# A fused attention and mixture kernel: first expert product in two halves, first steps and last outputs in another order

## The chip, the cores and the metric

The kernel runs on one core of a Trainium2 chip. Its time is the device time of one execution in microseconds; the median of several runs counts. TensorE (PE) multiplies, VectorE (DVE), ScalarE (ACT) and GpSimd (POOL) work on tiles, and SyncE (SP) issues the transfers. PEld is TensorE's loading of weights.

## What is computed

The reference is an attention with a narrow window and block summaries, followed by a soft mixture of experts on its output. Cut to what matters:

```python
# attention: 4 batches, 8 heads, 768 positions, head size 64; blocks of 32, window 16
k_sum = k.reshape(B, H, nb, block, D).max(axis=3)
v_sum = v.reshape(B, H, nb, block, D).mean(axis=3)
scores_l = scale * (q @ k^T), only where |i - j| < 16
scores_s = scale * (q @ k_sum^T) + log(32)
a = softmax(concat(scores_l, scores_s))
x = a @ concat(v, v_sum)                      # 3072 rows of 512

# mixture: 8 experts with 4 slots each, hidden size 1024
logits = x @ phi                              # 3072 x 32
slot_input = softmax(logits, axis=0).T @ x    # 32 x 512
h = relu(slot_input[e] @ w1[e])               # per expert, 4 x 1024
slot_out[e] = h @ w2[e]                       # 4 x 512
out = softmax(logits, axis=1) @ slot_out      # 3072 x 512
```

## The kernel before

Each engine executes its instructions in the order in which the program's text issues them; nothing reorders them. Engines wait for each other by semaphores.

The attention runs in 24 steps. A step is one third of the positions (256) of one half of a batch's heads; three steps share a key tile `kk` (two tiles, used in turn). Step i does the scores of step i on PE (line 234), their masked maxima on DVE (`soft_max`, line 253: eight operations that write p and its row maximum m), the exponentials on ACT (line 263, and line 265 after a subtraction on POOL, line 269), transposes (line 275) and their copies (line 280) for step i-1, and the product with v (line 291) for step i-2.

A key tile holds, beside the keys, the maxima of each block of 32 keys and the 16 keys at each edge. `k_max` forms the block maxima (DVE, line 187), `k_put` copies them into the tile (line 210), and `k_edge` copies the edges (line 203). The scores need all three. For the first tile k_put ran on DVE, for all others on POOL. `v_sum` (the words V0 to V7 of the table PLAN) sums v in blocks: 48 small products on PE (line 327), a copy `vp` on ACT and an addition into `vsst` on DVE (line 340). `put_v` then copies vsst into a v tile on POOL (line 350), and the product with v waits for that. PLAN says for each step which of such pieces are begun, ahead of the mark | within the step or behind it at its end.

`load_piece` transfers the expert weights, 512 KB each, 32 pieces of w1 and 32 of w2, into buffers as they come free, on SP's queue. From the sixth step on they run beside the attention.

Behind the attention the softmax over positions is finished (`lanes`, `slots`), and then the softmax over slots runs on DVE in two parts (lines 646 to 660), while PE multiplies with w1: 32 pieces of four products each into one result `hps` (line 667). The result is clipped at zero on DVE (`hs`), transposed on PE (`ph`, line 681) and copied into the two tiles W1ST and W2ST on DVE (line 683). Then comes w2 in three groups of columns: a (256), b and c (128 each). `stage2` is a generator: 16 steps of a or 8 of b or c on PE (line 705), the scaling `sos` on DVE (line 715), a product that adds up four parts (line 718) and a copy into `sls` on DVE (line 720). `combine` makes the outputs of a block of 128 columns from sls: A stands for the first two blocks, B for the third and C for the fourth. For each block it makes four products of 256 columns, copied by ACT and DVE into one 512 KB piece, and four of 512, copied into two pieces (lines 731, 742, 747), each then issued on SP's queue. The text END is the order at the end: each of its words advances one of these generators by one step; a digit is for reading only.

## Time and profile before

| | |
|---|---|
| median of three runs | 193.09 us (191.21 to 193.2) |
| the profiled execution | 191.26 us |
| its span | 189.0 us |
| PE busy | 165.9 us, 88% |
| DVE busy | 121.1 us, 64% |
| ACT busy | 94.4 us, 50% |
| POOL busy | 71.9 us, 38% |
| moved by DMA | 66.35 MB, 351 GB/s over the span |

The span runs from the first to the last instruction of the profiled execution; the time of an execution is longer by what lies around it. A share of busy time is a mean over stages that have different limits.

### The profile page before, as it was taken

The numbers are of one execution on the slowest core, as the hardware profiler recorded it, in microseconds if no ns is written. First come the engines' busy times: TensorE is split into PE (matmuls) and PEld (weight loads), VectorE is DVE, ScalarE is ACT, GpSimd is POOL, SyncE is SP. The second block draws the span as 40 slices with busy tenths as digits, with TensorE's granted clock in tenths as the row PEclk, the third lists the DMA queues.
The fourth block names the chain that finished last, engine by engine and source line by source line (L and its number), as shares of the span: only waits on it lengthen the run. The fifth ranks groups of instructions, "written<-read, shape, count | busy, mean of one in ns | idle before, by whom it ended". The sixth has DMA issues, their size and how long they took to land.

```text
span 189.0 us, 7987 instructions
## 1 busy us (share of the span) xinstructions
PE 165.9 (88%) x3201; PEld 130.0 (69%) x3201; DVE 121.1 (64%) x626; ACT 94.4 (50%) x244; POOL 71.9 (38%) x147
## 2 busy tenths in 40 slices
PE   6596999998999979899999898989779989998940
PEld 5394877976968967697798696878357755664720
DVE  1758599686879688848978885864567610135450
ACT  2026667587676677756678577765301000033240
POOL 3425956748544943824854844420020000000000
PEclk9969999999999999999999999999999999999985
DMA  5999989998799998979899999979999999999697
GB/s 193 415 401 400 344 336 299 385 393 312 223 368 386 304 355 262 352 231 297 290 264 389 402 408 408 388 275 394 416 409 404 402 413 408 406 401 396 251 397 269
DMA packets 20628, 66.35 MB, mean 351 GB/s; under 512 B 2288, under 2 KB 2288, under 8 KB 20592
## 3 DMA queue, kind: packets, MB, share of 16 engines
q1 hardware_dynamic: 20448, 65.48, 93.0%
q8 instruction: 25, 0.41, 0.9%
q10 hardware_dynamic: 144, 0.37, 0.5%
q14 instruction: 11, 0.09, 0.1%
HBM read 59.55 MB, written 6.29 MB: 348 GB/s over the span
## 4 chain that ended last, share of the span: by engine, by line
PE 55%; DVE 12%; ACT 12%; issue 4%; POOL 3%; DMA 2%; DVEq 1%; POOLq 0%; ACTq 0%; SPq 0%
PE s L234 8%; PE o L291 8%; PE pt L275 8%; PE hps L667 7%; PE so L705 6%; PE pp L327 5%; DVE p L253 5%; ACT xt L364 4%; PE pp L361 3%; ACT ptr L280 3%; PE op L731 3%; DMA out<-wa 2%; ACT p L263 2%; PE pp L374 2%; PE pp L417 2%
## 5 line engine op out<-in xcount | busy, mean ns | idle before, releaser
L263 ACT ACTIVATE p<-p,m 128x128 f32<-128x128 f32 x100 | 32.0, 391 | 27.3 <-DVE m L253 27.3
L253 DVE CUSTOM_DVE_ANT_0 p<-s,cs 128x128 f32<-128x128 f32 x192 | 42.6, 286 | 4.4 <-PE s L234 4.1
L269 POOL TENSOR_TENSOR p<-m,p 128x512 f32<-128x512 f32 x23 | 23.9, 1038 | 44.0 <-DVE m L253 28.1
L234 PE MATMUL s<-kk,q 64*64 64x128 f32 x768 | 29.9, 280 | 4.2 <-DVE kk L210 2.2
L350 POOL COPY v<-vsst 24x520 f32<-24x520 f32 x48 | 29.4, 612 | 4.4 <-issue 1.6
L234 PEld LDWEIGHTS s<-kk,q 64*64 64x64 f32 x768 | 24.0, 136 | 10.2 <-issue 4.7
L291 PE MATMUL o<-v,ptr 120*64 120x65 f32 (+1 forms) x768 | 27.9, 225 | 1.5 <-DVE x L312 0.9
L291 PEld LDWEIGHTS o<-v,ptr 120*64 120x64 f32 (+1 forms) x768 | 24.6, 138 | 5.6 <-issue 4.6
L275 PE MATMUL pt<-ident,p 128*128 128x128 f32 x192 | 27.9, 282 | 0.6 <-ACT p L265 0.2
L280 ACT COPY ptr<-pt 128x512 f32<-128x512 f32 x47 | 24.7, 571 | 1.7 <-PE pt L275 1.7
L275 PEld LDWEIGHTS pt<-ident,p 128*128 128x128 f32 x192 | 20.4, 140 | 6.2 <-issue 3.3
L187 DVE TENSOR_REDUCE ks<-kk 128x8 f32<-128x256 f32 x48 | 17.0, 410 | 4.3 <-DMA kk<-kx 4.2
L265 ACT ACTIVATE p<-p 128x512 f32<-128x512 f32 x23 | 14.7, 639 | 8.8 <-POOL p L269 8.7
L312 DVE TENSOR_TENSOR x<-o,z 128x256 f32<-128x256 f32 x48 | 18.1, 419 | 0.8
L253 DVE DVE_READ_ACCUMULATOR2_ANT m<- 128x1 f32 x192 | 15.9, 83 | 0.0
L327 PE MATMUL pp<-v,cs 64*64 64x128 f32 x384 | 14.0, 284 | 0.8 <-ACT xt L364 0.7
L327 PEld LDWEIGHTS pp<-v,cs 64*64 64x64 f32 x384 | 12.0, 141 | 1.6 <-ACT xt L364 1.2
L361 PE MATMUL pp<-ident,x 128*128 128x128 f32 x88 | 11.6, 273 | 0.1
L309 DVE TENSOR_SCALAR z<-o 128x8 f32<-128x8 f32 x24 | 4.0, 165 | 11.8 <-PE o L291 11.2
L364 ACT COPY xt<-pp 128x512 f32<-128x512 f32 x21 | 11.4, 595 | 0.0
L203 POOL COPY kk<-kk 128x192 f32<-128x192 f32 x32 | 9.6, 342 | 4.3 <-DMA kk<-kx 4.3
L742 ACT COPY wa<-op 128x256 f32<-128x256 f32 (+1 forms) x3 | 1.2, 445 | 20.0 <-PE op L731 20.0
(134 smaller groups left out, 199.9 us busy)
## 6 DMA issues: line engine op xcount, KB each, us to landing
wa<-w SPq DMA_DIRECT2D x40, 512.0 KB, 7.7
v<-vx SPq DMA_DIRECT2D x24, 520.0 KB, 6.1
kk<-kx SPq DMA_DIRECT2D x16, 400.0 KB, 5.3
q<-qx SPq DMA_DIRECT2D x24, 256.0 KB, 4.8
v<-w SPq DMA_DIRECT2D x7, 512.0 KB, 6.2
kk<-w SPq DMA_DIRECT2D x6, 512.0 KB, 6.9
x<-w SPq DMA_DIRECT2D x5, 512.0 KB, 7.5
out<-v SPq DMA_DIRECT2D x3, 512.0 KB, 4.8
```

Source lines behind the costliest of these rows:

```text
L234: nc.tensor.matmul(s[r][64 * c : 64 * c + 64, u, :].rearrange("p (a k) -> p a k", a=2), lhsT=qb[64 * r : 64 * r + 64, i % NQR, pr, o : o + ...
L253: nc.vector.tensor_tensor_reduce(out=p[:, u, :], in0=s[:, u, :], in1=maskv[:, mk, :], scale=-0.125, scalar=-NEG, op0=ALU.add, op1=ALU.min, ...
L263: nc.scalar.activation(out=p[:, u, :], in_=p[:, u, :], func=AF.Exp, scale=-1.0, bias=m[:, u : u + 1])
L269: nc.gpsimd.tensor_tensor(out=p, in0=m.unsqueeze(2).broadcast_to([128, 4, 128]), in1=p, op=ALU.subtract)
L275: nc.tensor.transpose(pt[:, u, :], p[:, u, :], ident)
L280: (eng or nc.scalar.copy)(out=ptr, in_=ptr_[i, r])
L291: nc.tensor.matmul(o[64 * c : 64 * c + 64, r, u, :], lhsT=ptr[0:K, u, 64 * c : 64 * c + 64], rhs=v[0:K, c, tt, 2 * pr + r, :], start=True, ...
L312: nc.vector.tensor_tensor(out=x[:, r], in0=o[:, r, :, 0:64].rearrange("p (t q) d -> p t q d", t=2), in1=z[:, r].rearrange("p (t q) -> p t ...
L327: nc.tensor.matmul(pv[c][64 * g : 64 * g + 64, 0:128].rearrange("p (h d) -> p h d", h=2), lhsT=cs[64 * c : 64 * c + 64, o : o + 64], rhs=v ...
L350: eng.tensor_copy(out=vs[i % NV][n0 : n0 + NB, c].rearrange("n t h c -> n t (h c)"), in_=src.broadcast_to([NB, 2, 260]))
L361: nc.tensor.transpose(pv[:, 128 * c : 128 * c + 128], x, ident)
L364: (nc.vector.tensor_copy if on_dve else nc.scalar.copy)(out=xt.rearrange("p c t -> p (c t)"), in_=pv)
```

## The change

At the start, the first key tile's block maxima are copied for two of six tiles of positions by DVE and for four by POOL, ahead of POOL's memset of W1ST. The q tile of step 1 is loaded ahead of the first v tiles. V0 moves from the end of step 0 into step 1; the put_v of the first v tile follows it. The block maxima of the second key tile move to the end of step 1 and into step 2, and k_put and k_edge of that tile follow POOL's subtraction of step 2.

At the experts, the product with w1 is split into experts 0 to 3 and 4 to 7. Each half has its own result and is clipped, transposed and copied by a generator `hidden`. The first half's transposes stand behind the 20th piece, the second half's behind the fourth step of a (the new word h in END). The second part of the softmax over slots moves behind the 20th piece. In END, block B's outputs begin before the last three steps of c.

```diff
--- before.py
+++ after.py
@@ -39,7 +39,7 @@
 
 
 PLAN = {
-    0: "| V0",
+    1: "V0 |",
     2: "| V1",
     5: "| V2",
     6: "X0 X1 |",
@@ -66,8 +66,8 @@
 
 CHUNKS = {"a": (0, 256), "b": (256, 128), "c": (384, 128)}
 END = (
-    "a a a a a a a a a a a a a a a a a1 b b a2 b b a3 b b A A b A A b A A c A A c b1 c b2 c b3 c "
-    "c c c c1 B c2 c3 B B B C C C C"
+    "a a a a h a a a a a a a a a a a a a1 b b a2 b b a3 b b A A b A A b A A c A A c b1 c b2 c b3 c B c B c "
+    "B c c1 B c2 c3 C C C C"
 )
 
 
@@ -202,13 +202,14 @@
                 src = bass.AP(src.tensor, src.offset, [src.ap[0], src.ap[1], [128, NTT], [1, 16]])
                 eng.tensor_copy(out=e[:, :, :, 16 * half : 16 * half + 16], in_=src)
 
-    def k_put(hb, eng):
+    def k_put(hb, eng, t0=0, n=NTT):
         if hb >= HB:
             return
         for c in range(2):
             o = 0 if c else 32
             eng.tensor_copy(
-                out=eview(hb, c)[:, :, :, o : o + NB], in_=kst[hb].unsqueeze(2).broadcast_to([128, 2, NTT, NB])
+                out=eview(hb, c)[:, :, t0 : t0 + n, o : o + NB],
+                in_=kst[hb].unsqueeze(2).broadcast_to([128, 2, n, NB]),
             )
 
     def keys(hb, r, c, pr, t):
@@ -508,9 +509,9 @@
     load_k(0, 1)
     load_q(0)
     nc.scalar.dma_start(out=cs, in_=cst)
+    load_q(1)
     for i in range(TPS):
         load_v(i)
-    load_q(1)
     load_q(2)
     load_k(1, 0)
     load_k(1, 1)
@@ -523,7 +524,8 @@
     for part in range(6):
         k_max(0, part)
     k_edge(0, nc.gpsimd)
-    k_put(0, nc.vector)
+    k_put(0, nc.vector, 0, 2)
+    k_put(0, nc.gpsimd, 2, 4)
     nc.gpsimd.memset(W1ST, 0.0)
 
 
@@ -548,19 +550,31 @@
         soft_max(i, 0)
         soft_exp(i, 0)
         flush(held)
-        if a >= 0:
+        if a > 0:
             for c in range(2):
                 put_v(a, c, nc.gpsimd)
         for n in range(LOADS[i]):
             if now[0] < 19:
                 load_piece(True)
-        if tp == 2:
+        if tp == 2 and hb > 0:
             k_put(hb + 1, nc.gpsimd)
         soft_max(i, 1)
         if i < NSTEP - 1:
             soft_sub(i, 1)
-        if tp == 1:
+        if i == 1:
+
+            flush(begin(front))
+            front = ""
+            put_v(0, 0, nc.gpsimd)
+            put_v(0, 1, nc.gpsimd)
+        if i == 2:
+            for part in (3, 4, 5):
+                k_max(1, part)
+            k_put(1, nc.gpsimd)
+        if tp == 1 and hb > 0:
             k_edge(hb + 1, nc.gpsimd)
+        if i == 2:
+            k_edge(1, nc.gpsimd)
         if a >= 0:
             trans(a, 0)
             trans(a, 1)
@@ -571,7 +585,10 @@
         if b >= 0:
             values(b)
             norm(b)
-        if tp < 2:
+        if i == 1:
+            for part in (0, 1, 2):
+                k_max(1, part)
+        if tp < 2 and hb > 0:
             for part in ((0, 1, 2), (3, 4, 5))[tp]:
                 k_max(hb + 1, part)
         held = begin(back)
@@ -643,7 +660,7 @@
 
 
 
-    for q0, n in ((0, 4), (4, 2)):
+    def row_softmax(q0, n):
         l = lt[:, q0 : q0 + n].rearrange("p q t -> p (q t)")
         ct = fin.tile([128, 512], F32, name="ct", bufs=1)[:, 0 : 128 * n]
         cv = ct.rearrange("p (b s) -> p b s", s=NE * 4)
@@ -659,31 +676,44 @@
         nc.vector.tensor_tensor(out=cv, in0=cv, in1=cz.unsqueeze(2).broadcast_to([128, 4 * n, 32]), op=ALU.mult)
         nc.vector.transpose(out=l, in_=ct)
 
-    hps = pf.tile([128, 512], F32, name="hps", tag="pf")[:, 0:256]
+
+    def hidden(h):
+        hs = fin.tile([128, 2, 128], F32, name="hs", tag="hs", bufs=2)
+        for i in range(2):
+            nc.vector.tensor_scalar_max(out=hs[:, i, :], in0=hps[h][:, 128 * i : 128 * i + 128], scalar1=0.0)
+        yield
+        ph = po.tile([128, 512], F32, name="ph", tag="op")
+        for i in range(2):
+            nc.tensor.transpose(ph[:, 128 * i : 128 * i + 128], hs[:, i, :], ident)
+        yield
+        for i in range(2):
+            nc.vector.tensor_copy(
+                out=W2ST[i].rearrange("p j (e k) -> p j e k", e=NE)[:, :, 4 * h : 4 * h + 4, 0:4],
+                in_=ph[:, 128 * i : 128 * i + 128].rearrange("p (j e k) -> p j e k", j=4, e=NE)[:, :, 4 * h : 4 * h + 4],
+            )
+
+    row_softmax(0, 4)
+    hps, hid = [], [hidden(0), hidden(1)]
     for k in range(32):
         _, e, c = pieces[k]
         t = wt[k].rearrange("p (j f) -> p j f", j=4)
+        if k % 16 == 0:
+            hps.append(pf.tile([128, 512], F32, name="hps", tag="pf")[:, 0:256])
         for j in range(4):
             nc.tensor.matmul(
-                hps[32 * j : 32 * j + 32, :],
+                hps[-1][32 * j : 32 * j + 32, :],
                 lhsT=W1ST[:, c, 32 * e : 32 * e + 32],
                 rhs=t[:, j, :],
-                start=(k == 0),
-                stop=(k == 31),
+                start=(k % 16 == 0),
+                stop=(k % 16 == 15),
                 tile_position=(0, 32 * j),
             )
         load_piece()
-    hs = fin.tile([128, 2, 128], F32, name="hs", tag="sos", bufs=1)
-    ph = pf.tile([128, 512], F32, name="ph", tag="pf")
-    nc.vector.tensor_scalar_max(out=hs[:, 0, :], in0=hps[:, 0:128], scalar1=0.0)
-    nc.vector.tensor_scalar_max(out=hs[:, 1, :], in0=hps[:, 128:256], scalar1=0.0)
-    for i in range(2):
-        nc.tensor.transpose(ph[:, 128 * i : 128 * i + 128], hs[:, i, :], ident)
-    for i in range(2):
-        nc.vector.tensor_copy(
-            out=W2ST[i].rearrange("p j (e k) -> p j e k", e=NE)[:, :, :, 0:4],
-            in_=ph[:, 128 * i : 128 * i + 128].rearrange("p (j e k) -> p j e k", j=4, e=NE),
-        )
+        if k % 16 == 15:
+            advance(hid[k // 16])
+        if k == 19:
+            flush(hid[0:1])
+            row_softmax(4, 2)
 
 
     first = {}
@@ -754,7 +784,10 @@
     st2 = {name: stage2(name) for name in CHUNKS}
     comb = {name.upper(): combine(name) for name in CHUNKS}
     for n in END.split():
-        advance(comb[n] if n in comb else st2[n[0]])
+        if n == "h":
+            flush(hid[1:])
+        else:
+            advance(comb[n] if n in comb else st2[n[0]])
     flush([*st2.values(), *comb.values()])
```

POOL at the start, before. Names are out<-in; kk_84 is the first key tile and kk_85 the second, v_87 to v_89 the first v tiles, p_99 and p_100 the two buffers of p.

```order
L203 COPY kk_84<-kk_84 128x12x16 x4
L527 MEMSET W1ST 128x1152
L269 TENSOR_TENSOR p_99<-m,p_99 128x512
L350 COPY v_87<-vsst 24x520 x2
L269 TENSOR_TENSOR p_100<-m,p_100 128x512
L203 COPY kk_85<-kk_85 128x12x16 x4
L350 COPY v_88<-vsst 24x520 x2
L210 COPY kk_85<-ks 128x12x24 x2
L269 TENSOR_TENSOR p_99<-m,p_99 128x512
```

POOL at the same place in the changed kernel:

```order
L203 COPY kk_84<-kk_84 128x12x16 x4
L210 COPY kk_84<-ks 128x2x4x24 x2
L529 MEMSET W1ST 128x1152
L270 TENSOR_TENSOR p_99<-m,p_99 128x512
L270 TENSOR_TENSOR p_100<-m,p_100 128x512
L351 COPY v_87<-vsst 24x520 x2
L351 COPY v_88<-vsst 24x520 x2
L270 TENSOR_TENSOR p_99<-m,p_99 128x512
L210 COPY kk_85<-ks 128x12x24 x2
L203 COPY kk_85<-kk_85 128x12x16 x4
```

Two copies of the first tile's block maxima came ahead of the memset, and the second tile's two groups of copies moved behind the third subtraction (that of step 2).

PE at the start, before, from the last scores of step 0 on (s_169 is a result of step 0, s_236 and s_237 those of step 1):

```order
L234 MATMUL s_169<-kk_84,q 64x128 x2
L327 MATMUL pp<-v_87,cs 64x128 x8
L327 MATMUL pp<-v_88,cs 64x128 x8
L327 MATMUL pp<-v_89,cs 64x128 x8
L234 MATMUL s_236<-kk_84,q 64x128 x2
L234 MATMUL s_237<-kk_84,q 64x128 x2
```

And in the changed kernel, where s_208 and s_209 are the results of step 1:

```order
L235 MATMUL s_209<-kk_84,q 64x128 x2
L328 MATMUL pp<-v_87,cs 64x128 x8
L328 MATMUL pp<-v_88,cs 64x128 x8
L328 MATMUL pp<-v_89,cs 64x128 x8
L276 MATMUL pt<-ident,p_99 128x128 x8
L235 MATMUL s_292<-kk_84,q 64x128 x2
```

V0's products stood between the scores of steps 0 and 1 and now stand behind both.

DVE at the end, before, from the last step of b's result on. sos is the scaled sum, sls its copy; the outputs kk_84, v_92 and x_96 are the third block's.

```order
L720 COPY sls<-so_3110 128x128
L715 TENSOR_SCALAR sos<-so,rz 128x128
L720 COPY sls<-so_3165 128x128
L747 COPY kk_84<-op 128x256 x2
L747 COPY v_92<-op 128x512
L747 COPY x_96<-op 128x512
L747 COPY q<-op 128x256 x2
```

And in the changed kernel:

```order
L750 COPY sls<-so_3121 128x128
L777 COPY kk_84<-op 128x256 x2
L745 TENSOR_SCALAR sos<-so,rz 128x128
L777 COPY v_92<-op 128x512
L777 COPY x_96<-op 128x512
L750 COPY sls<-so_3193 128x128
L777 COPY q<-op 128x256 x2
```

The third block's first two copies moved ahead of the scaling of c, and its other two stand between that scaling and the copy of c into sls.

## Rows read from the trace of the kernel before

**Rows 1.** Busy time by stretches: engines' us, then clock, DMA share, GB/s.

```profile
122.00:130.00 8.00, 7.11 (x151) 6.09 (x149) 5.10 (x29) 5.04 (x14) 2.00 (x4) 1.00 0.89 315
130.00:177.00 47.00, 43.27 (x780) 28.71 (x773) 19.58 (x53) 7.85 (x22) 1.06 (x1) 1.00 1.02 407
177.50:180.00 2.50, 2.50 (x18) 1.95 (x18) 2.01 (x5) 1.66 (x5) 0.00 (x0) 1.00 0.32 126
```

**Rows 2.** Start, us; DVE's copies by line (min/median/max ns), then the timeline around them.

```profile
L210 DVE COPY kk<-ks x2: 291/834/1377, 7.6 to 8.9; 128x288 f32<-128x288 f32 x2
...
6.57 1.20 POOL L203 COPY kk<-kk 128x192 f32<-128x192 f32 x4 [4.31 <-DMA kk<-kx]
7.72 1.06 POOL L527 MEMSET W1ST<- 128x1152 f32 x1
9.04 2.02 PE L234 MATMUL s<-kk,q 64*64 64x128 f32 x29 [2.21 <-DVE kk L210]
```

**Rows 3.** Stretches of the scores of steps 0 and 1; POOL's first subtraction.

```profile
9.04:11.27 2.23, 2.23 (x39) 2.17 (x43) 0.11 (x1) 0.00 (x0) 0.00 (x0) 0.52 1.03 392
13.02:14.30 1.28, 1.28 (x43) 1.11 (x35) 0.96 (x5) 0.09 (x1) 1.04 (x1) 1.00 1.04 409
...
13.14 1.04 POOL L269 TENSOR_TENSOR p<-m,p 128x512 f32<-128x512 f32 x1 [4.36 <-DVE m L253]
```

**Rows 4.** Timelines of POOL, PE and DVE from step 1 to step 3.

```profile
17.63 1.04 POOL L269 TENSOR_TENSOR p<-m,p 128x512 f32<-128x512 f32 x1 [0.56 <-DVE m L253]
18.61 1.20 POOL L203 COPY kk<-kk 128x192 f32<-128x192 f32 x4
19.88 1.28 POOL L350 COPY v<-vsst 24x520 f32<-24x520 f32 x2
21.11 0.79 POOL L210 COPY kk<-ks 128x288 f32<-128x288 f32 x2
...
21.05 1.54 PE L327 MATMUL pp<-v,cs 64*64 64x128 f32 x48
22.41 1.05 PE L234 MATMUL s<-kk,q 64*64 64x128 f32 x32
...
23.75 0.58 DVE L340 TENSOR_TENSOR vsst<-pp,vp 24x128 f32<-24x128 f32 x2 [1.38 <-ACT vp L337]
24.36 0.29 DVE L253 CUSTOM_DVE_ANT_0 p<-s,cs 128x128 f32<-128x128 f32 x1
```

**Rows 5.** The transfer of v tile 5, issued at 11.7 us.

```profile
DMA to landing us min/median/max: 9.1/9.1/9.1
```

**Rows 6.** The chain that ended last: transposes in a step, and the seam of the products.

```profile
36.15 1.02 PE pt L275 x8
...
140.90 14.05 PE hps L667 x256
...
155.32 0.54 PE ph L681 x2
...
156.23 7.99 PE so L705 x160
```

**Rows 7.** Third block's outputs issued at 178.82 and at 179.70, in this order.

```profile
DMA to landing us min/median/max: 2.6/2.6/2.6
...
DMA to landing us min/median/max: 3.1/3.1/3.1
```

**Rows 8.** Timeline of PE and of DVE around the third block's outputs.

```profile
171.02 1.14 PE L731 MATMUL op<-lt,sls 32*128 32x512 f32 x8
176.63 0.71 PE L731 MATMUL op<-lt,sls 32*128 32x256 f32 x8
...
176.77 0.35 DVE L715 TENSOR_SCALAR sos<-so,rz 128x128 f32<-128x128 f32 x1 [2.06 <-PE so L705]
178.00 0.75 DVE L747 COPY kk<-op 128x256 f32<-128x256 f32 x2
178.94 0.69 DVE L747 COPY v<-op 128x512 f32<-128x512 f32 x1 [0.19 <-PE op L731]
```

## The prediction, made before the result

> **What bounds the kernel now.** I read the busy time by stretches first, because one share over the whole span hides which stage is limited by what [rows 1]. From 130 to 177 us the DMA engines are busy all the time and move 407 GB/s, so that stretch is bounded by bytes: no engine work that ends earlier there ends the kernel earlier. There are two holes in the stream. Between 122 and 130 us the DMA share is 0.89, and between 177.5 and 180 us it is 0.32. The second hole is 0.68 of 2.5 us, so 1.7 us of transfer time, and it stands directly before the last output pieces. The reader should see in it the one place of the tail where an earlier output can pay.
>
> Before about 120 us the DMA rate is lower and the engines set the pace, each step handing over to the next; nothing in a step waits for the clock on the wall. If the first steps end earlier or later, I take it that the whole rest moves by as much, since the stream of weight pieces is fed by buffers that the steps release.
>
> The profiled execution took 191.26 us with a span of 189.0, so 2.3 us lie around the span, which the change doesn't touch. The three runs before have a median of 193.09 (191.21 to 193.2). I make the sum against the profiled execution and put the difference on the median.
>
> **The start, step by step.** DVE writes the block maxima into the key tile in two copies. One takes 0.291 us, the other 1.377 us [rows 2]. The long one starts at 7.6, while POOL is in its copies on line 203 (6.57, 1.20 us, so to 7.77), and it stays open while POOL's memset of W1ST runs (7.72, 1.06 us, so to 8.78). TensorE's first score product starts at 9.04, behind it. So at this place DVE's copy doesn't run beside POOL; it waits about 1.09 us.
>
> The change leaves DVE two smaller copies (tiles 0 and 1) and gives POOL two copies for the other four, ahead of the memset. What decides is when DVE gets its turn. Such copies of 192 columns take POOL 0.30 us each (1.20 us for the four on line 203). If DVE gets in when POOL's line 203 ends (7.77), its two copies are done by 7.77 + 2 x 0.29 = 8.35. If it gets in one or two POOL copies later, 8.65 or 8.95. If it loses every handover up to the memset's end, 7.77 + 2 x 0.30 + 1.06 = 9.43, plus 0.2, and scores start at 9.55, 0.5 us later than now. The trace shows one such handover, and DVE lost it, to an instruction that only writes. The new POOL copies read as well, and DVE has to lose three handovers in a row to come out worse than now. I take 8.65 (0.4 us earlier), and keep 8.35 and 9.55 as ends.
>
> [...]
>
> Next in the chain: scores of step 0 take 2.23 us at a granted clock of 0.52 and 1.28 us (those of step 1) at the full one [rows 3]; the half clock is granted after TensorE was idle from 6.84 to 9.04. Then eight masked maxima, 1.87 us from the end of the scores at 11.27 to the subtraction on POOL at 13.14 that waits for them; I count 1.8 and 0.1 for the handover. The change puts the scores of step 1 directly behind those of step 0 and moves V0's 48 products behind them, and it takes the block maxima of block 1 and V0's sum out of DVE's way to the maxima of step 1. From 8.65: 10.9 (slow scores), 12.7 (maxima 0), 13.95 (scores 1), 15.8 (maxima 1 and handover), where POOL's subtraction can begin; it begins at 17.63 now [rows 4].
>
> From there POOL has, in the new order, a subtraction 1.04, two pairs of put_v 2 x 1.28, the second subtraction 1.04, k_put 0.79 and k_edge 1.20: 6.63 us, back to back. So the keys of block 1 are complete at 15.8 + 6.6 = 22.4. They are complete at 21.9 now, since POOL does only k_edge, one put_v pair and k_put after its subtraction (21.11 + 0.79). (DVE keeps up with that: after maxima 1 at 15.7 come V0's sum, 0.6, three block maxima, about 1.1, and maxima 2, 1.8, so 19.2, and POOL wants those at 15.8 + 3.6 = 19.4; the last three block maxima then lie beside the second subtraction.) This is the wait that the change adds: k_put and k_edge now stand behind the second subtraction, and scores of step 3 stand behind them on TensorE. They start at 22.41 now and at about 22.4 then.
>
> A second bound lies at the same time. V1's products need v tile 5, which was issued at 11.7 and landed 9.1 us later, at 20.8 [rows 5]; the DMA stream is full up to there, so it will not land earlier by much. V1 starts at 21.05 now, right behind that. 20.8 + 1.54 = 22.35. Whatever is won before, step 3 can't start its scores much before 22.4.
>
> What is still won lies behind it: DVE's maxima of step 3 start at 24.36, about 0.9 us after their scores end, because the sums of V1 (23.75, 0.58 us) stand first and wait for ACT, which is held up by POOL's second subtraction: that stands behind k_put now (21.9 to 22.9). In the new order it is done by 20.5, ACT is free at V1's end, and the maxima can start at 22.4 + 1.05 + 0.1 = 23.55. The start is worth 24.36 - 23.55 = 0.8 us. Its ends are -0.9 (all of it) and, if scores start at 9.55, the rival below. The split of load_q(1) ahead of the v tiles costs nothing: q tile 1 is 256 KB of the same stream, V0 needs its three v tiles later than before, and if V0 were to wait the cover is the maxima of step 0 (1.8 us).
>
> **The first product.** Now TensorE ends the product at 154.95 and starts the next at 156.23: 1.28 us in which the result is clipped, transposed and copied, all of it on the chain [rows 6]. Afterwards the first half's transposes stand behind 20 pieces and the second half's behind four steps of the next product, which needs only experts 0 to 3 up to there; a step is 0.44 us (7.99 us for 16 steps of a and 2 of b), four are 1.8, more than the 0.35 us between the product's end and the transposes now, so DVE's part is hidden. The cost is twice two transposes, 0.54 us a pair as they stand in the chain; in a run of eight they take 1.02, so 0.26 a pair at best. 1.28 - 2 x 0.54 = 0.2 us earlier, with ends 0.76 earlier and, if each switch costs 0.2 us more, 0.2 later. The second softmax over rows moves on DVE behind piece 20; DVE had nothing else to do up to the product's end, and the result is first wanted by the outputs after product a, so it costs nothing. If it ran late, DVE's clipping of the second half would be late next, under the same 1.8 us. None of this is on the DMA stream, which is full; it counts only through the last outputs.
>
> **The order at the end.** The third block's first output (256 columns) now waits for all steps of c: its piece is issued at 178.82 and lands 2.6 us later, the next is issued at 179.70 and lands 3.1 us later [rows 7]. In the new order these four products (0.71 us, from 176.63 now) come three steps of c earlier: 176.63 - 3 x 0.44 - 0.2 = 175.1, to 175.8, and with DVE's two copies (0.75) their piece is issued at about 176.6, before the queue is empty at 177.5. A piece of 512 KB is 1.28 us at 407 GB/s and goes into the hole. But the block's second part (four products of 512 columns, 1.14 us) now stands on DVE behind sos of c, which waits for the last step of c. TensorE's chain to that step grows by 0.71 + 1.14 us of products and shrinks by 0.2: sos at about 178.4 instead of 176.77, then 0.35, then two copies of 0.69 [rows 8]. The piece behind the first copy is issued at about 179.6, just as now (179.70), and sls of c follows both copies at about 180.2, 2.4 us later than now; the last block's outputs are then late by about 1 us at the issue, under the two pieces on the wire. So a hole remains, about from 178.8 to 181, and the gain is only that the second piece finds an empty queue: 2.6 instead of 3.1 us to land, 0.45 us, and the 0.2 of the first product. I take 0.65; the ends are 0.1 (DVE later by half a microsecond) and 1.7 (the hole closes).
>
> **Sum.** 0.8 + 0.65 = 1.45 us earlier: 189.8 for the profiled execution, 191.6 on the median.
>
> **Rivals.** First, POOL keeps DVE out to the memset's end, but the clock comes back as it did (at about 12.6): scores at 9.55, maxima 0 from 11.8, scores of step 1 at 13.5, subtraction at 16.6, keys of block 1 at 23.2, maxima of step 3 at 24.35, as now. Only the tail is left: 193.09 - 0.65 = 192.4. For it speaks the one handover in the trace; against it, that three are needed.
> Second, and on the other side: the same, and TensorE, which now has gaps between the scores of steps 0 and 1 where V0's products stood, stays at the half clock through scores 1 and V0. Scores 1 then end 0.95 us later (2.23 for 1.28) and V0's products later too, put_v and with it POOL's whole chain are late by as much, and maxima of step 3 start between 25.25 and 25.75: 0.9 to 1.4 us lost, less the tail's 0.65: about 193.6, up to 194.5. It decides once POOL's first subtraction of step 1 begins after 16.7, since 6.6 us of POOL and the 1.05 us of scores then end after 24.36.
> Third, everything pays: hole closed (1.7) and start 0.9: 190.5. For it speaks that DVE's copies may drain sooner than I place them; against it, the order of sos before them.
>
> **How the numbers follow.** Forecast 0.5 (191.6), first rival 0.25 (192.4), second 0.13 (193.6), third 0.12 (190.5). One per cent is 1.9 us, about what a measurement of this kernel can tell from no change: faster means under 191.16, slower over 195.0. The third case and a quarter of the forecast's own spread lie under the first bound: 0.25. Only the end of the second rival and its unknowns reach the other: 0.06. The range leaves out half of the outer cases: 190.2 to 193.9; the three runs before are 2 us apart by themselves, which this width also has to hold.
>
> **What would show it.** In the new profile: the first score product before 9.0 (else a rival), DVE's two small copies under 0.6 us together, maxima of step 3 near 23.5, V1 at about 20.8; no gap of 1.28 us at the seam of the two products; a third-block output issued near 176.6, and a hole in the DMA of about 2 us that moved to 179 and didn't vanish. Wrong would make it: a step in the middle that doesn't pass on the shift, or V1 no longer bound by its tile.

## The result, and the profile after

The changed kernel takes 191.09 us (median of 20 runs, 189.48 to 192.38) against 192.97 us before (20 runs, 190.84 to 194.96): ratio 0.9903, with 0.9878 to 0.9927 as 95% interval, that is 1.9 us faster, between 1.4 and 2.4. The forecast was 191.6, and 1.45 us faster.

One profiled execution alone would have said the opposite: the changed kernel's took 191.62 us (span 189.8), the one before 191.26. So the trace is read stretch by stretch. The start first: this is the timeline of the changed kernel (start, duration, engine, line; in brackets the idle time ahead and what ended it).

```profile
7.53 0.57 DVE L210 COPY kk<-ks 128x96 f32<-128x96 f32 x2
7.70 0.63 POOL L210 COPY kk<-ks 128x192 f32<-128x192 f32 x2
7.92 1.43 PE L235 MATMUL s<-kk,q 64*64 64x128 f32 x32 [1.67 <-DVE kk L210]
8.28 1.06 POOL L529 MEMSET W1ST<- 128x1152 f32 x1
...
11.27 1.71 PE L235 MATMUL s<-kk,q 64*64 64x128 f32 x26 [0.30 <-DVE m L254]
14.69 1.04 POOL L270 TENSOR_TENSOR p<-m,p 128x512 f32<-128x512 f32 x1 [2.44 <-DVE m L254]
16.44 2.63 POOL L351 COPY v<-vsst 24x520 f32<-24x520 f32 x4 [0.70 <-POOL p L270]
19.49 1.04 POOL L270 TENSOR_TENSOR p<-m,p 128x512 f32<-128x512 f32 x1 [0.42 <-DVE m L254]
20.47 0.79 POOL L210 COPY kk<-ks 128x288 f32<-128x288 f32 x2
21.02 0.67 PE L328 MATMUL pp<-v,cs 64*64 64x128 f32 x16 [0.49 <-DMA v<-vx]
21.20 1.22 POOL L203 COPY kk<-kk 128x192 f32<-128x192 f32 x4
22.48 1.20 PE L235 MATMUL s<-kk,q 64*64 64x128 f32 x30 [0.15 <-POOL kk L203]
23.60 0.29 DVE L254 CUSTOM_DVE_ANT_0 p<-s,cs 128x128 f32<-128x128 f32 x1 [0.91 <-PE s L235]
24.62 1.15 PE L292 MATMUL o<-v,ptr 120*64 120x65 f32 x32
25.82 0.17 DVE L310 TENSOR_SCALAR z<-o 128x8 f32<-128x8 f32 x1 [0.45 <-PE o L292]
27.91 0.28 DVE L254 CUSTOM_DVE_ANT_0 p<-s,cs 128x128 f32<-128x128 f32 x1
```

DVE's two copies take 0.57 us together (the first alone took 1.38 before, [rows 2]), and scores start at 7.92 instead of 9.04, earlier than the best end of the prediction. The maxima of step 3 start at 23.60 (24.36 before, [rows 4]). But then DVE waits 0.45 us for a product of TensorE at 25.82, and the maxima of step 4 are only 0.22 us earlier than in the kernel before, whose rows there are these:

```profile
24.42 1.15 PE L291 MATMUL o<-v,ptr 120*64 120x65 f32 x32
26.05 0.16 DVE L309 TENSOR_SCALAR z<-o 128x8 f32<-128x8 f32 x1
28.13 0.28 DVE L253 CUSTOM_DVE_ANT_0 p<-s,cs 128x128 f32<-128x128 f32 x1
```

Next the granted clock, from the busy time by stretches (engines' us; then clock, DMA share, GB/s) of the changed kernel:

```profile
11.30:13.00 1.70, 1.70 (x35) 1.70 (x38) 0.17 (x1) 0.63 (x1) 0.95 (x1) 0.52 1.06 416
136.00:141.00 5.00, 3.38 (x34) 2.20 (x37) 3.17 (x12) 0.41 (x2) 0.45 (x1) 1.00 1.04 414
141.00:144.50 3.50, 3.50 (x36) 2.22 (x37) 2.63 (x4) 0.63 (x1) 0.62 (x1) 0.51 1.01 400
```

and, in the kernel before, the last two of these stretches:

```profile
136.00:141.00 5.00, 3.38 (x34) 2.20 (x37) 3.17 (x12) 0.41 (x2) 0.44 (x1) 1.00 1.03 415
141.00:144.50 3.50, 3.50 (x68) 2.57 (x71) 2.64 (x4) 0.63 (x1) 0.63 (x1) 1.00 1.02 404
```

TensorE is busy for 3.38 of 5 us up to 141 in both. Then one execution is granted the half clock (0.51 over the stretch) and the other the full one (1.00), and the product of w1 does 36 instead of 68 products in the same 3.5 us. That is why the profiled execution of the changed kernel was no faster. It isn't the change: in the experiments below, kernels with the old start or the old product of w1 have it too.

The seam, from the chain that ended last in the changed kernel: two pairs of transposes of 0.37 us stand where 1.28 us stood ([rows 6]).

```profile
140.88 10.53 PE hps L703 x160
151.41 0.37 PE ph L687 x2
...
158.82 0.37 PE ph L687 x2
```

The end, from the timeline of the changed kernel, and behind it two stretches of the busy time, whose last two columns are the stream's:

```profile
176.49 0.71 PE L761 MATMUL op<-lt,sls 32*128 32x256 f32 x8
177.26 0.76 DVE L777 COPY kk<-op 128x256 f32<-128x256 f32 x2 [1.39 <-PE op L761]
179.92 0.35 DVE L745 TENSOR_SCALAR sos<-so,rz 128x128 f32<-128x128 f32 x1 [1.91 <-PE so L735]
180.19 0.68 DVE L777 COPY v<-op 128x512 f32<-128x512 f32 x1
180.94 0.33 SPq L781 DMA_DIRECT2D out<-v  x1
181.39 0.28 DVE L750 COPY sls<-so 128x128 f32<-128x128 f32 x1
```

```profile
177.50:180.00 2.50, 2.35 (x52) 1.13 (x41) 0.59 (x3) 1.06 (x4) 0.00 (x0) 1.00 0.84 331
180.00:182.00 2.00, 0.74 (x6) 0.58 (x10) 1.67 (x4) 0.37 (x1) 0.00 (x0) 1.00 0.27 109
```

The whole end is 1.17 us later than before, since the half clock came ahead of it (first output product at 167.83 instead of 166.66). Against that product, the third block's piece v is issued 13.1 us later, as before (179.70 - 166.66 = 13.0, [rows 7]), and the hole in the stream stands right ahead of it. The hole moved and didn't vanish, as forecast, and the piece landed 2.6 us behind its issue, where it took 3.1 before ([rows 7]):

```profile
DMA to landing us min/median/max: 2.6/2.6/2.6
```

### The profile page after: what moved, and what is told of

Same layout as the page of the kernel before. It is cut to its first block, busy times and chain, and to the rows that moved or that the text cites. A ratio compares the mean times of both kernels' runs of the same rounds, so it can differ in the third digit from the quotient of the medians.

```text
span 189.8 us, 7996 instructions
## 1 busy us (share of the span) xinstructions
PE 167.5 (88%) x3203; PEld 128.2 (68%) x3203; DVE 120.7 (64%) x630; ACT 94.9 (50%) x244; POOL 72.7 (38%) x149
## 4 chain that ended last, share of the span: by engine, by line
PE 59%; DVE 13%; ACT 11%; POOL 6%; issue 5%; DMA 3%; SPq 0%; POOLq 0%; ACTq 0%; DVEq 0%
PE s L235 10%; PE hps L703 8%; PE so L735 7%; PE pt L276 7%; PE o L292 7%; DVE p L254 5%; PE pp L328 4%; PE op L761 4%; ACT xt L365 4%; ACT ptr L281 3%; DMA kk<-kx 3%; ACT p L264 3%; PE pp L362 3%; PE pp L375 2%; PE pp L418 2%
## 5 line engine op out<-in xcount | busy, mean ns | idle before, releaser
L276 PE MATMUL pt<-ident,p 128*128 128x128 f32 x192 | 27.2, 281 | 0.7 <-ACT p L266 0.5
L703 PE MATMUL hps<-wa,W1ST 128*32 128x256 f32 x168 | 11.2, 428 | 0.5 <-DVE rz L472 0.5
(133 smaller groups left out, 189.8 us busy)
```

The lines of the kernel that those rows point to most:

```text
L276: nc.tensor.transpose(pt[:, u, :], p[:, u, :], ident)
L703: nc.tensor.matmul(hps[-1][32 * j : 32 * j + 32, :], lhsT=W1ST[:, c, 32 * e : 32 * e + 32], rhs=t[:, j, :], start=(k % 16 == 0), stop=(k % ...
```

## Experiments

Single executions differ by more than a part of the change is worth, so beside the ratios I use three marks of each trace: the first maxima of step 4 (what the start leaves), the time from the first product of w1 to the first output product (the seam), and from there to the span's end. Every run also has a time of the kernel before on the same chip; the runs were spread over several chips, so two of them are best compared by their ratios.

| kernel | ratio to before | maxima of step 3 | of step 4 | w1 to output | output to end | half clock granted, us |
|---|---|---|---|---|---|---|
| before | 1 | 24.36 | 28.13 | 25.76 | 22.33 | 9.14 to 12.56 |
| changed | 0.9903 | 23.60 | 27.91 | 26.94 | 21.96 | 11.36 to 14.78, 141.07 to 144.48 |
| start alone | 0.9921 | 23.36 | 27.67 | 27.45 | 22.31 | 10.88 to 14.29, 140.59 to 144.00 |
| halves alone | 0.9961 | 24.43 | 28.21 | 26.94 | 22.29 | 9.13 to 12.54, 142.25 to 145.66 |
| end alone | none | 24.43 | 28.55 | 27.17 | 21.97 | 141.59 to 145.00 |
| changed, filled at 136 | 0.9809 | 22.31 | 26.43 | 25.26 | 21.95 | none |
| before, filled at 136 | 0.9883 | 24.86 | 28.95 | 25.76 | 22.29 | 8.64 to 12.05, 18.88 to 22.29 |
| edge copies early | 0.9788 | 22.65 | 26.97 | 25.26 | 22.48 | 11.41 to 14.83 |
| start filled too | 0.9759 | 22.18 | 26.49 | 25.26 | 21.94 | none |
| c first | 0.983 | 22.87 | 26.96 | 25.26 | 22.88 | none |
| block B first | 0.9812 | 22.69 | 26.97 | 25.26 | 21.89 | none |
| memset first | one run | 25.21 | 29.53 | 26.94 | 22.06 | 9.93 to 16.75, 143.05 to 146.46 |
| memset later | one run | 24.53 | 28.61 | 27.46 | 22.28 | 18.46 to 21.87, 141.34 to 144.75 |
| before, filled twice | 0.9941 | 24.11 | 28.20 | 25.76 | 22.29 | 17.58 to 20.99 |

(The half clock granted after 179 us, up to the span's end, is left out of the last column.)

**Start alone.** Only the start's parts of the diff.

> Kernel before with the new start alone (experts and end as before). My theory, that a part counts by what still stands ahead of the slots product: maxima of step 3 at about 23.6 us as in the changed kernel's trace (24.36 before), but the values of that step only 0.2 earlier, so step 20 about 0.4 us earlier and the whole 0.2 to 0.5 us faster (ratio 0.998). As predicted before the result (the whole 0.8 passes on): ratio 0.996. Rival, that the start's gain is lost by the first expert product, since it began at 140.88 in the changed kernel and at 140.90 before: ratio 1.000.

Measured: 191.93 against 193.50 us, ratio 0.9921 (0.9881 to 0.9961). The start pays, more than I expected, and the rival (1.000) falls; step 20 was 0.68 us earlier in this execution. Of the start's parts only the memset and the edge copies are tested further below; V0's new place and the q tile ahead of the v tiles weren't tried by themselves.

**Halves alone.** `hidden`, the two halves with the later second softmax, and the word h in END.

> Kernel before with the first product in two halves alone. My theory: the 1.28 us seam becomes two pairs of transposes of 0.44 to 0.54 us, so the last outputs are issued 0.2 to 0.5 us earlier; ratio 0.998. Rival, that the full DMA stream hides it: ratio 1.000 within 0.1 us, with a larger hole in the stream before the last outputs closed by as much.

Measured: 192.90 us, ratio 0.9961 (0.9921 to 1.0002). The interval doesn't exclude the rival; the marks do better. The time from w1 to the first output product without half clock is 25.76 with one product and 25.26 with two halves, in every trace: 0.50 us. The rest behind it keeps its length (22.3), so the gain arrives.

**End alone.** Only the last line of END and its neighbour.

> Kernel before with the new order of the third block's outputs alone. My theory, from the changed kernel's trace, where the last block's outputs are issued 0.4 us earlier than the shift of the stretch before lets one expect: 0.4 us faster, ratio 0.998, with a hole in the DMA stream between 178 and 181 us. The prediction had 0.45. Rival, that the copies ahead of the scaling of c make the last block late by as much as the new place of the first piece gives: ratio 1.000 or above.

Measured: median 192.94 against 193.50 us over six runs, which spread from 189.31 to 194.99, too wide for a ratio. The mark decides: output to end is 22.28 to 22.33 with the old order (six traces) and 21.94 to 21.97 in four of the six with the new one (22.06 and 22.48 in the other two): 0.35 us. In the trace with 22.48 (edge copies early) piece v landed 3.5 us behind its issue instead of 2.6, which I read as a queue that wasn't empty, and this gain was missing. The profiled execution is late in the middle for another reason, a wait of TensorE between products of values at which the trace names no releaser:

```profile
34.76 0.28 PE L291 MATMUL o<-v,ptr 128*64 128x65 f32 x2 [0.79 <-issue]
```

**Changed kernel with filled waits.** Four products on constants, which nobody reads, in the waits between 136 and 141 us; the output is unchanged.

```diff
+    def fill(n):
+        if not spare:
+            spare.append(ps_s.tile([128, 4, 128], F32, name="s0"))
+        nc.tensor.matmul(spare[0].rearrange("p u k -> p (u k)")[:, 0:n],
+            lhsT=ident, rhs=cs[:, 0:n], start=True, stop=True)
...
         nc.tensor.transpose(pv[0:1, 0:128], stat[...], ident)
+        fill(256)
+        fill(128)
...
         nc.tensor.matmul(pc[:, 0:1], lhsT=f..., rhs=one11, ...)
+        fill(256)
...
                 pi[:, c, :], lhsT=acc[...], rhs=ps["R"][:, 0:32], start=True, stop=True
             )
+        fill(256)
```

> The changed kernel with TensorE given extra products that nobody reads (five, 128x256 or 128x128, on constants, into an unused PSUM tile) in the waits between 136 and 141 us; the output is unchanged. My theory, that the times fall into two groups because the granted clock falls to half at 141 us in some executions and not in others: the upper group goes, the median falls by 0.7 to 1.3 us against the changed kernel (ratio to before about 0.985) and the clock of most runs is 0.98 or more. Rival, that the clock at that place isn't set by TensorE's idle time there, or the groups come from elsewhere: ratio 0.990 as without the extra products, two groups as before.

(The edit has four products, where this text counts five.) Measured: 189.31 us (188.59 to 190.77), ratio 0.9809 (0.975 to 0.9868). By the medians that is 1.8 us less than the changed kernel, about as much again as the change. In its trace TensorE is busy for 4.93 us of the stretch and keeps the clock (1.00):

```profile
136.00:141.00 5.00, 4.93 (x54) 3.34 (x57) 3.14 (x11) 0.31 (x1) 1.06 (x1) 1.00 1.03 411
141.00:144.50 3.50, 3.50 (x72) 2.57 (x68) 2.58 (x6) 0.63 (x1) 0.00 (x0) 1.00 1.02 407
```

Of the seven traces without the extra products, six have the half clock between 140.6 and 146.5; of the seven with them, none. It costs 1.4 to 1.7 us (w1 to output 27.17 to 27.46 for 25.76, and 26.94 for 25.26). This execution also had the full clock at the start, and there V1's last products waited for v tile 5 alone, as the prediction's second bound has it:

```profile
20.61 0.67 PE L328 MATMUL pp<-v,cs 64*64 64x128 f32 x16 [1.72 <-DMA v<-vx]
21.10 1.09 PE L235 MATMUL s<-kk,q 64*64 64x128 f32 x32
```

**Kernel before with filled waits.** The same `fill` in the kernel before.

> The kernel before with the same five extra products between 136 and 141 us as in the run with the filled waits; output unchanged. My theory, that the half clock near 141 us costs both kernels about 1.5 us in the executions that have it, and that the change's worth is its three parts: the ratio to before is 0.991 to 0.994, and the changed kernel with the extra products (189.31 us) is still 1.2 to 1.8 us faster than this one. Rival, that what the change gains is mainly fewer executions with the half clock there: this kernel comes within 0.6 us of 189.3.

Measured: 191.62 us, ratio 0.9883 (0.983 to 0.9936); the products gave this kernel more than I expected. The changed kernel with the same products is 1.4 us faster by the ratios, whose intervals overlap, and 2.3 by the medians; 1.2 to 1.8 was expected. Between these two traces, both at full clock from 136 us to the last products (1.00 in the stretches up to 144.5), the seam is 0.50 and the end 0.34 us shorter. So the change's worth isn't a smaller number of executions with the half clock at 141; the rival falls.

**Edge copies early.** In the filled changed kernel, `k_edge(1)` moved ahead of `put_v(0, 0)`.

> The changed kernel with the extra products at 136 to 141 us, and with the edge copies of the second key tile put on POOL before put_v of the first v tiles instead of behind the third subtraction. My theory, that scores of step 3 wait for these copies when the scores of step 1 ran at half clock (22.42 us in the changed kernel's trace), but for v tile 5 when they ran at the full one (20.6 us in the trace with the extra products): at most 0.6 us earlier at step 4 in executions of the first kind and nothing in the second; ratio 0.978 to 0.981. Rival, that the second subtraction and the values, now behind the edge copies, come later by as much: ratio 0.982 or above.

Measured: 189.03 us, ratio 0.9788 (0.9737 to 0.9838). With the half clock at the start, maxima of step 3 came at 22.65, 0.95 us earlier than in the changed kernel, of step 4 at 26.97, 0.94 earlier (0.7 earlier than with the start alone, which had the half clock too). So in such an execution the wait that the change adds (k_edge behind the subtraction) does cost, by this one trace more than the 0.6 us I expected; the median can't be told from the filled kernel's.

**Start filled too.** Ten products instead of seven ahead of the first scores, and three behind them.

```diff
-    for _ in range(7):
+    for _ in range(10):
...
         if i == 0:
+            for _ in range(3):
+                nc.tensor.matmul(wm[:, 0:256], lhsT=acc[:, 0:128], rhs=acc[:, 0:256], ...)
```

> The changed kernel with the extra products at 136 to 141 us, and with more of them at the start: ten instead of seven before the first scores, three between the scores of steps 0 and 1. My theory, that the half clock for scores of step 1 and V0 (granted from 11.36 to 14.78 us in the changed kernel's trace) is what makes keys of block 1 complete at 22.4 instead of 20.9: full clock up to 20 us, scores of step 3 at 21.1 right behind V1, which waits for v tile 5; step 4 at about 26.4 (27.9 in the changed kernel), ratio 0.976 to 0.979. Rival, that TensorE's extra work delays scores of step 1 or the clock falls all the same: ratio 0.981 or above.

Measured: 188.20 us (187.84 to 189.88), ratio 0.9759 (0.9712 to 0.9805), the lowest time here, though the intervals of the two filled kernels above overlap it. Maxima of step 4 (26.49) are no earlier than in the filled kernel (26.43), whose execution had the full clock at the start without these products. Scores of step 3 stand right behind V1, and that behind its tile:

```profile
20.36 0.67 PE L328 MATMUL pp<-v,cs 64*64 64x128 f32 x16 [1.41 <-DMA v<-vx]
20.85 1.41 PE L235 MATMUL s<-kk,q 64*64 64x128 f32 x32
```

**Block B or c first.** Two orders of DVE at the end; PE's order is unchanged. The first is in the filled kernel, the second in the one with the filled start.

```diff
-    "B c c1 B c2 c3 C C C C"
+    "B c c1 c2 c3 B C C C C"      # c first
+    "B c B c1 c2 c3 C C C C"      # block B first
```

> The changed kernel with the extra products at 136 to 141 us, and with the last scaling and copy of c (sos, second product, sls) ahead of DVE's two copies of the third block's second part. My theory, that the last block waits for these two copies (sls begins 1.3 us after sos ends in the trace): its outputs are issued 0.4 to 0.6 us earlier, the third block's second and third pieces 0.6 us later, and since the queue is empty at that time the end moves little: ratio 0.979 to 0.982. Rival, that the last block alone sets the end: 0.5 us faster, 0.978.

> The kernel with the filled start and the extra products at 136 to 141 us, and with DVE's two copies of the third block's second part ahead of the scaling of c instead of behind it (the other way round from the run with c first). My theory after that run, that the piece which ends the hole in the DMA stream sets the end and the last block doesn't: that piece is issued 0.8 us earlier (12.3 us after the first output product instead of 13.1), the last block's pieces 0.4 us later, and the end comes 0.3 to 0.7 us earlier against the first output product (21.94 us in the run with the filled start): ratio to before 0.973 to 0.975. Rival, that the last block, issued later, takes over: 21.9 us or more, ratio 0.976 or above.

Measured: with c first 190.14 us, ratio 0.983 (0.9789 to 0.9871), output to end 22.88 instead of 21.95. Piece v is issued 0.9 us later and the end is 0.9 us later, though the last block's piece q is issued earlier (180.18 - 164.88 = 15.3 us behind the first output product, 15.5 without the edit). I had expected the end to move little, and the rival had it earlier; both fall, since the hole ahead of piece v decides. The timeline and the stretches show the hole getting longer:

```profile
178.92 0.33 SPq L794 DMA_DIRECT2D out<-v  x1
```

```profile
177.50:178.50 1.00, 0.62 (x6) 0.42 (x10) 0.53 (x2) 0.00 (x0) 0.00 (x0) 1.00 0.25 102
178.50:180.00 1.50, 1.50 (x13) 0.91 (x15) 1.50 (x4) 0.65 (x2) 0.00 (x0) 0.99 0.21 85
```

With B first, 189.30 us, ratio 0.9812 (0.9757 to 0.9867), output to end 21.89: piece v is issued at 177.67, 12.3 us behind the first output product, 0.8 earlier, and nothing is won, since the last block's pieces come later (its q at 181.04, 15.6 behind). My theory that only the hole's end counts falls on this side, and the rival holds; the order of the change stands between two bounds. The time is 1.1 us above that of the kernel with the filled start; not by the end, which differs by 0.05, but maxima of step 4 (0.5 us) and the middle (0.9 us) were later in this execution.

**Memset first, memset later.** In the changed kernel POOL's memset of W1ST ahead of its two `k_put` copies; and in the kernel before the memset behind the subtraction of step 0.

```diff
+    nc.gpsimd.memset(W1ST, 0.0)      # first: changed kernel
     k_put(0, nc.gpsimd, 2, 4)
-    nc.gpsimd.memset(W1ST, 0.0)
...
+        if i == 0:                   # later: kernel before, behind soft_sub(i, 1)
+            nc.gpsimd.memset(W1ST, 0.0)
```

> The changed kernel with POOL's memset of W1ST ahead of its two copies of the first key tile's block maxima instead of behind them. Theory of the memset, that in the trace of before it was the memset that held DVE's copy open (1.377 us) and that copies of POOL don't: DVE's second copy ends about when the memset ends, near 8.8 us, first scores at 8.9 or later. The prediction's theory, that every POOL instruction keeps DVE out alike: the same 8.8, but then DVE's copies beside POOL's would have been held in the changed kernel too, and there they took 0.28 and 0.37 us. Rival, that only size decides (288 columns against 96): copies of 0.28 and 0.37 us here too, first scores at 7.9 us.

> The kernel before with POOL's memset of W1ST moved behind the subtraction of step 0 and nothing else. Theory of the memset: DVE's two copies of 288 columns take about 0.3 to 0.4 us each, first scores at 8.1 to 8.3 us instead of 9.04. Rival, that a copy of 288 columns is slow beside POOL's copies or by itself: about 1.4 us for the first as before, first scores at 9.0.

Measured, with the memset first: both DVE copies stay open, though they have 96 columns (the line's instructions, min/median/max ns), and in the timeline the maxima of step 3 are late.

```profile
L210 DVE COPY kk<-ks x2: 1136/1210/1284, 7.7 to 7.9; 128x96 f32<-128x96 f32 x2
```

```profile
7.73 1.33 DVE L210 COPY kk<-ks 128x96 f32<-128x96 f32 x2
7.89 1.06 POOL L528 MEMSET W1ST<- 128x1152 f32 x1
...
25.21 0.29 DVE L254 CUSTOM_DVE_ANT_0 p<-s,cs 128x128 f32<-128x128 f32 x1 [1.63 <-PE s L235]
```

With the memset later, copies of 288 columns are short too, the first of them beginning beside POOL's copies of line 203 (6.92 to 8.12 us):

```profile
L210 DVE COPY kk<-ks x2: 292/334/375, 7.9 to 8.2; 128x288 f32<-128x288 f32 x2
```

```profile
8.39 1.25 PE L234 MATMUL s<-kk,q 64*64 64x128 f32 x29 [2.02 <-DVE kk L210]
```

So the memset is what held DVE's copy for over 1 us, and size alone doesn't explain it. But POOL's copies hold DVE as well, for less time. In the changed kernel, instruction by instruction:

```profile
7.41 0.34 POOL L203 COPY kk<-kk 128x192 f32<-128x192 f32 x1
7.53 0.28 DVE L210 COPY kk<-ks 128x96 f32<-128x96 f32 x1
7.70 0.34 POOL L210 COPY kk<-ks 128x192 f32<-128x192 f32 x1
```

DVE's first copy ends 0.06 us behind the POOL copy beside which it began, and the second (7.73, 0.374 us) 0.06 us behind the next POOL copy (8.04). This is so (0.06 to 0.07 us) for all 14 such copies in the seven traces that have them, and with the memset first the first copy ends 0.06 us behind the memset too. Copies of 288 columns end 0.16 us behind the memset in five traces, and 0.16 us behind the last copy of line 203 with the memset later. The second of these copies, with no POOL instruction beside it, takes 0.29 us ([rows 2]), less than a third of the columns beside POOL (0.37). So my expectation misread the 0.28 and 0.37 us as copies that weren't held: the traces look like a turn at the end of each POOL instruction, as the prediction had it. DVE got its turn ahead of POOL's next copy, but not ahead of the memset.

Each of the two has one time (193.08 and 192.42 us), which tells little. With the memset later, first scores 0.65 us earlier than before brought nothing at step 4 (28.61 for 28.13), in an execution with the half clock from 18.46.

**Kernel before, filled twice.** The kernel before with filled waits and ten products at the start.

> The kernel before with the extra products at 136 to 141 us and ten instead of seven ahead of the first scores; output unchanged. It holds the clock away from both places, so that against the kernel with the filled start (188.2 us, ratio 0.976) it shows what the three parts of the change are worth at full clock. My theory: the seam of the product costs 0.50 us, the order at the end 0.35 us as in the traces so far, and the start at full clock 1.0 to 1.8 us at step 4 (it was 0.2 to 0.5 us with the half clock at the start): this kernel is 1.9 to 2.6 us slower than 188.2, at 190.1 to 190.8 us, ratio 0.984 to 0.988. Rival, that the start's gain is TensorE's clock alone, so that a filled start gives the old order the same: 189.0 to 189.6 us, ratio 0.978 to 0.981.

Measured: 191.19 us, ratio 0.9941 (0.9896 to 0.9986); 3.0 us slower by the medians, 3.5 by the ratios, than the changed kernel with the filled start (which has three more products behind the first scores), more than expected. The rival's 189.0 to 189.6 us falls. But the products didn't hold the clock: in this execution the half clock came at 17.58 instead, and maxima of step 4 at 28.20, as without them. The only trace of the old start with the full clock up to step 4 is that of the end alone (step 4 at 28.55), and there TensorE waited 1.17 us among V1's products for nothing that the profile shows:

```profile
22.12 1.20 PE L327 MATMUL pp<-v,cs 64*64 64x128 f32 x34 [1.17 <-issue]
```

So what the old order would gain from a clock that stays full isn't shown.

## Why the prediction was right, step by step

- **The copies at the start.** Direction and mechanism were right, the size too small. DVE's copies did take turns with POOL's instructions, as far as the trace shows it, and got both turns early: they ended 0.06 us behind POOL's last copy of line 203 (7.75) and behind its first `k_put` copy (8.04). I charged each copy the 0.29 us of 288 columns and let scores wait for both, where the first (done at 7.82) is enough: they start at 7.92 instead of 8.65 (8.35 to 9.55). The order of the turns the traces don't settle: in the changed kernel and with the memset first alike, DVE's copy had begun 0.16 us ahead of POOL's next instruction, while POOL was still in line 203, and it came ahead of the copy but behind the memset. What decides isn't shown.
- **Rival 2's mechanism is real.** The half clock through scores 1 and V0, which I had tied to late scores, came with early ones (11.36 to 14.78), behind waits of TensorE for the maxima of step 0 (1.19 and 0.30 us). The filled kernel (1.22 and 0.27 us) and the run with c first have the same two waits and kept the full clock, so they don't decide alone. By the point I gave (POOL's subtraction after 16.7) it shouldn't decide, and at 14.69 it didn't. With the memset first, scores at 9.11 and the half clock up to 16.75, maxima of step 3 start at 25.21, at the lower end of what the rival had (25.25 to 25.75). But the subtraction began at 15.95 there, before that point; what came late was put_v (18.07), behind V0's sum. (By its own terms the rival's time was 193.3 to 193.8 us, not up to 194.5.)
- **The chain to step 3.** Keys of block 1 complete at 22.4 (21.20 + 1.22), forecast 22.4; maxima of step 3 at 23.60, forecast 23.55. That is luck in part. POOL's subtraction began 1.1 us earlier than forecast (14.69 for 15.8), but the 6.63 us behind it weren't back to back: POOL waited 0.70 us ahead of put_v, for V0's sum (done on DVE at 16.32; V0's products ran at the half clock), and 0.42 us ahead of the second subtraction, for the maxima of step 2.
- **The step that failed: "The start is worth 24.36 - 23.55 = 0.8 us"**, with the bound behind it and passed on whole. I put all 48 products of V1 (1.54 us) behind v tile 5 and so let no scores of step 3 start much before 22.4. Only the last 16 (0.67 us) wait for that tile: in executions of the new start with the full clock there, scores of step 3 start at 20.9 to 21.7, maxima of step 3 at 22.2 to 22.9 and of step 4 at 26.4 to 27.0. And the shift isn't passed on whole. In the changed kernel's profiled execution 0.76 became 0.22 at step 4, because TensorE's products for step 3 (scores, transposes, values) were 0.2 later than before, and DVE, no longer late itself, then waited for them. I followed DVE past the point and not TensorE. Over the four traces with the new start and no edit there (27.91, 27.67, 26.43, 26.96) the mean is 27.2, against 28.4 over the five with the old one (28.13, 28.21, 28.55, 28.95, and 28.20 with three more products ahead): 1.2 us, where 0.8 stood, from few traces that spread by 1.5 and 0.8 us. Between executions with one half-clock stretch in the first steps (27.91 and 27.67 against 28.13 and 28.21) it is 0.2 to 0.5 us. The rest stands on two executions of the new start with the full clock and on three of the old with a second stretch, a later one, or a wait of 1.17 us, so how much of it is the order stays open. Why the clock falls there in some executions only isn't shown.
- **The middle passes the shift on.** From maxima of step 4 to the product of w1 the traces have 112.3 to 113.6 us whatever the kernel (112.76 before, 112.97 changed, 112.31 start alone, 113.56 end alone). The 0.2 us of the changed kernel was lost in this spread, to which waits like the one of 0.79 us above belong; what decides when they occur stays open.
- **The seam**: 0.2 forecast (0.76 to -0.2), 0.50 measured: I charged 0.54 us for each pair of transposes, and between products they take 0.37.
- **The end**: 0.45 forecast, 0.35 measured, by the step as written: the hole moves, piece v is issued at the same place (0.07 us later) and finds an empty queue (a DMA share of 0.27 from 180 to 182 us; 2.6 us to landing for 3.1).
- **The other rivals**: the first (start worth nothing, 192.4) falls with the run of the start alone; the third (190.5) had the hole closed, and it is there.
- **The sum** is 1.2 + 0.50 + 0.35 = 2.0 us, for 1.9 measured; forecast 0.8 + 0.2 + 0.45. Start (on average) and seam were both sized too low, so nothing cancelled, and the forecast fell 0.4 us short, well inside its range.
- **What no step had**: the half clock at 141 us. It stands in six of the seven traces without extra products, of old and new code, so I read no part of the difference from it, but it makes the profiled execution of before (191.26, without it) probably untypical of its median (193): of the 1.8 us that I only carried over as a difference, the 1.4 to 1.7 that it costs are likely the larger part. There is no second trace of the kernel before that could show it.

## What to carry to other kernels

When a step ahead of a hand-over gets earlier, follow every engine that takes part in the next step, not only the one that was late: the gain ends where the second latest stands. Where executions of one kernel differ by as much as an edit is worth, compare stretches between fixed marks in many traces; twelve runs of the halves left open by their ratio what the mark showed alike in every trace. And look what the clock does behind sparse stretches of TensorE: here the half clock came near 141 us in six of seven executions, behind a stretch that was busy for 3.38 of 5 us in the changed kernel, and four products there that nobody reads were worth about as much as the whole change (1.8 us by the medians, and 1.9).

## What the runs showed of the hardware

- In these traces a DVE copy of line 210 that begins while POOL writes or copies stays open until a POOL instruction ends, and ends 0.06 to 0.07 us (96 columns; 0.11 us for the second copy behind the memset put first) or 0.16 us (288 columns) behind it: 0.28 to 0.38 us long behind POOL's strided copies, 1.14 to 1.38 us behind a memset of 1152 columns, also when DVE started 0.16 us ahead of the memset.
- The half clock was granted at 140.6 to 143.1 us in six of seven executions without the extra products and in none of seven with them. TensorE was busy for 3.38 of the 5 us up to 141 in the changed kernel, which was granted the half clock, and in the kernel before, which kept the full one; with the extra products for 4.93 to 4.97. At the start, more products ahead don't rule it out: it came at 17.58 in the last run. With the old code at the start it varies between executions: at 9.14 us in the kernel before, at 8.64 and again at 18.88 in the same with filled waits, and not at all there with the end alone.
- Between products of values at 32 to 35 us TensorE waited 0.24, 0.49, 0.64 and 0.79 us in four traces (filled at 136, block B first, before filled twice, end alone) for nothing that the profile shows, and not in others. What it waits for stays open.
